# Local attention and a gated feed-forward block on one core: turns of x one tile ahead, turns of a batch inside its steps, output sums by thirds across tiles

## Chip, cores, metric

One core of one Trainium2 chip. The metric is the device time of that core in microseconds (us); quoted times are medians over the fast runs of a kernel, with their range. Unless another label is named, times inside an execution come from one profiled execution of each kernel, counted from its first instruction.

## The reference, cut to what matters

```python
# q, k, v: (8, 8, 576, 64) = batch, heads, rows, head width; 8 global positions
scores = q @ k.T / 8
mask = (abs(i - j) <= 32) | is_global[i] | is_global[j]
attn = softmax(where(mask, scores, -1e9))
x = (attn @ v).transpose(0, 2, 1, 3).reshape(4608, 512)
g = x @ w_gate                       # 512 -> 1536
val = x @ w_val
res_gate = sigmoid(x @ w_res)
out = x + res_gate * ((gelu(g) * val) @ w_out)
```

The kernel works through the 4608 rows in nine chunks of 512. While it runs the feed-forward block of chunk c, it computes the attention of chunk c+1. Each chunk has twelve steps j (a g product, a v product, Gelu, their product), then four output tiles of 128 rows. Rows of q and k are turned (transposed) before the scores; rows at the global positions are fetched by a gather with a list of indices. PSUM is where matmuls leave their results; a copy brings them out. In the traces, pt are the exponentials of the scores, masked by VectorE (DVE); ob is an output tile and prb the product that it is made from.

## The kernel before

The start of chunk 0. A step's products are begun for 128 rows as soon as that tile of x is turned:

```python
    values(0, 2)
    turn_x(0, 0)
    values(0, 3)
    begin(0)                       # g and v of steps 0 and 1 for 128 rows: 16 short matmuls
    for t in range(1, 4):
        turn_x(0, t)               # 4 transposes on TensorE into PSUM, one copy out
        begin(t)
```

GpSimd's list inside chunk 0 (issued at step 5) and the turns of batch 1:

```python
                    for n in (12, 13): cast_piece(n, POOL)      # pieces of the weights, f32 to bf16
                    for c5 in range(5): cast_v(1, c5, POOL)
                    for n in range(16, 20): load_piece(n)
                    for i, n in enumerate(range(14, 20)):
                        cast_piece(n, POOL)
                        if i % 2: shift_on_chip(i // 2)         # two GpSimd copies of v, moved by 64 rows
                    shift_on_chip(3)
                if 7 <= j < 11:
                    for what in "kq": turn_pair(1, j - 7, what) # behind step j, not inside it
```

The output tiles. `work_f[4*t]` is the gate of tile t, `work_f[4*t+1..3]` its thirds; the last third also makes the output:

```python
        def third(n):
            def emit():
                ...                                     # 4 of the 12 matmuls of f_ps
                if n == 2:
                    prb = work.tile([128, 512], F32, name="prb", tag="prb")   # the pool gives 2 buffers
                    nc.vector.scalar_tensor_tensor(prb, held["r"], 1.0, held["f"], ALU.add, ALU.mult)
                    ob = work.tile([128, 512], F32, name="ob", tag="ob")      # 2 buffers, too
                    nc.gpsimd.tensor_tensor(ob, prb, xtok[c % 2][:, t, :], ALU.add)
                    nc.sync.dma_start(out[r0:r0 + 128, :], ob)                # on SyncE's queue
```

The end of chunk 0, and the start of chunk 1:

```python
            load_second("k"); load_second("q")     # 10 loads of batch 2 on SyncE's queue
            ...
            work_f[3]()                            # output tile 0
            cast_second("q", 0, 1, POOL)
            values(1, 3)
            work_f[7]()                            # output tile 1
            cast_second("q", 1, 3, POOL)
            turn_qk(2, "k")                        # 5 DMA transposes on SyncE's queue
            turn_x(1, 2)
            work_f[9](); work_f[10]()
            turn_x(1, 3)
            work_f[11]()                           # output tile 2
            cast_second("q", 3, NQT, POOL)
            for n in (13, 14, 15): work_f[n]()     # output tile 3
    # chunk 1
            turn_qk(b, "q" if c == 1 else "qk")    # 5 DMA transposes on SyncE's queue
            load_v(b)                              # 5 DMAs issued by GpSimd
            if c in (1, 2, 4):
                for what in "kqv":
                    gather(what, c // 2 + 1)       # issued by GpSimd, behind load_v
    # chunk 1, steps 8 to 11
                    if j == 8: double_qk(n0, n1)   # casts of the gathered rows: kgd, qgd
                    elif j == 9:
                        got = turn_globals(n0, n1) # TensorE turns them: tg
                if j == 11: held = global_scores(b)   # sg
```

The softmax here doesn't subtract the row's maximum and nothing guards it: scores larger than these inputs give would overflow.

## Time and profile before

| | before |
|---|---|
| median of fast runs, us | 398.69 (397.61 to 399.43, 4 runs) |
| PE idle, 14 to 50 us | 4.03 |
| PE idle, 50 to 90 us | 1.91 |
| PE idle, 90 to 100 us | 0.21 |

The idle times are the length of a stretch less TensorE's (PE's) busy time in it, from the table by stretches.

### The profile page before, as it was taken

How to read it: one execution, taken by the hardware profiler on the slowest of the kernel's cores; microseconds unless marked ns; L12 is line 12 of the kernel's file. 1: busy time of each engine (PE TensorE's matmuls, PEld its weight loads, DVE VectorE, ACT ScalarE, POOL GpSimd, SP SyncE). 2: the span in 40 equal slices, each digit the busy share in tenths (PEclk: the TensorE clock that was granted, in tenths of full speed). 3: DMA queues.
4: the chain of work that ended last, by engine and by line, in shares of the span. 5: the costliest groups of instructions: out<-in, count | busy, mean ns of one | idle time of the engine just before them, and what ended most of it. 6: DMA issues, size and time to landing. Idle time of an engine off the chain costs nothing.

```text
span 396.5 us, 8446 instructions
## 1 busy us (share of the span) xinstructions
PE 376.3 (95%) x3309; PEld 196.4 (50%) x3360; DVE 204.2 (51%) x445; ACT 168.4 (42%) x279; POOL 172.1 (43%) x207
## 2 busy tenths in 40 slices
PE   3969998999999999999999999999999999999995
PEld 2655555444554455445544554455445544554443
DVE  7747668346643463456434553555445534553322
ACT  5744593236333643355234623372337233633320
POOL 7778678758247514461385226712501210121011
PEclk9999999999999999999999999999999999999999
DMA  8999999799439943998299929993990310041002
GB/s 241 222 360 366 246 337 212 164 162 176 59 109 155 189 58 99 119 202 85 79 156 161 115 81 115 194 108 86 112 147 16 80 55 0 2 96 52 0 29 79
DMA packets 153002, 52.78 MB, mean 133 GB/s; under 512 B 136386, under 2 KB 143426, under 8 KB 152962
## 3 DMA queue, kind: packets, MB, share of 16 engines
q1 hardware_dynamic: 77024, 41.88, 45.1%
q0 software_dynamic: 75392, 9.84, 42.4%
q8 instruction: 26, 0.43, 0.5%
q10 hardware_dynamic: 546, 0.52, 0.4%
q14 instruction: 14, 0.11, 0.1%
HBM read 39.19 MB, written 9.44 MB: 123 GB/s over the span
## 4 chain that ended last, share of the span: by engine, by line
PE 81%; DMA 5%; issue 5%; ACT 3%; DVE 3%; POOL 2%; SPq 0%; ACTq 0%; DVEq 0%; POOLq 0%
PE v_ps L618 21%; PE g_ps L618 21%; PE f_ps L661 20%; PE r_ps L636 6%; PE nd L563 4%; PE sc L523 2%; PE nd L575 2%; DMA qgf<-in_q_dram,idx 2%; DMA kt<-k_st 2%; DMA ht<-in_q_dram 1%; PE ss L477 1%; ACT pt L530 1%; POOL ob L667 1%; POOL ve L99 1%; DVE pt L545 1%
## 5 line engine op out<-in xcount | busy, mean ns | idle before, releaser
L625 DVE SCALAR_TENSOR_TENSOR ht<-gsb,v_ps 128x512 bf16<-128x512 bf16 x108 | 74.1, 687 | 97.4 <-PE v_ps L618 91.6
L624 ACT ACTIVATE gsb<-g_ps 128x512 bf16<-128x512 f32 x108 | 64.4, 597 | 125.5 <-PE g_ps L618 117.5
L667 POOL TENSOR_TENSOR ob<-prb,xtok 128x512 f32<-128x512 f32 x35 | 40.4, 1153 | 176.3 <-DVE prb L665 174.7
L618 PE MATMUL v_ps<-xt,wv_t 128*128 128x512 bf16 (+1 forms) x456 | 111.9, 368 | 0.4
L618 PE MATMUL g_ps<-xt,wg_t 128*128 128x512 bf16 (+1 forms) x438 | 109.6, 367 | 2.5 <-ACT xt L599 1.3
L661 PE MATMUL f_ps<-wo_t,ht 128*128 128x512 bf16 x395 | 97.8, 379 | 1.9 <-issue 1.0
L618 PEld LDWEIGHTS <-wg_t 128*128 128x128 bf16 x456 | 43.3, 98 | 50.6 <-issue 2.7
L618 PEld LDWEIGHTS <-wv_t 128*128 128x128 bf16 x456 | 43.5, 98 | 49.9
L661 PEld LDWEIGHTS <-ht 128*128 128x128 bf16 x420 | 38.8, 98 | 38.6
L639 ACT ACTIVATE rsb<-r_ps 128x512 bf16<-128x512 f32 x36 | 21.7, 607 | 71.0 <-PE r_ps L636 69.9
L530 ACT ACTIVATE pt<-sc 128x512 bf16<-128x512 f32 x72 | 37.5, 623 | 4.6 <-PE sc L523 4.6
L665 DVE SCALAR_TENSOR_TENSOR prb<-rsb,f_ps 128x512 f32<-128x512 bf16 x35 | 24.0, 686 | 28.4 <-PE f_ps L661 25.9
L636 PE MATMUL r_ps<-wr_t,xt 128*128 128x512 bf16 x136 | 36.2, 379 | 0.5
L545 DVE TENSOR_TENSOR pt<-pt,maskw 128x512 bf16<-128x512 bf16 x64 | 29.8, 481 | 8.1 <-ACT pt L530 6.1
L91 POOL DMA_DIRECT2D q_st<-in_q_dram x25 | 21.4, 866 | 19.6 <-DMA qt<-q_st 19.1
L563 PEld LDWEIGHTS <-pt 128*128 128x128 bf16 x576 | 22.0, 97 | 10.2 <-DVE pt L545 0.9
L99 POOL DMA_DIRECT2D ve<-in_v_dram x30 | 25.5, 864 | 0.0
L588 DVE TENSOR_TENSOR xtok<-nd,rden 128x512 bf16<-128x512 f32 x34 | 23.5, 692 | 1.3
L563 PE MATMUL nd<-ve,pt 128*128 128x65 bf16 x320 | 22.7, 193 | 0.6 <-DVE xtok L588 0.6
L91 POOL DMA_DIRECT2D k_st<-in_k_dram x25 | 21.1, 865 | 4.3 <-DMA kt<-k_st 3.4
L587 DVE RECIPROCAL rden<-nd 128x8 f32<-128x8 f32 x34 | 7.0, 207 | 28.1 <-PE nd L575 27.9
L563 PE MATMUL nd<-vo,pt 128*128 128x65 bf16 x256 | 20.1, 193 | 1.0 <-DVE pt L545 0.6
(166 smaller groups left out, 291.9 us busy)
## 6 DMA issues: line engine op xcount, KB each, us to landing
out_dram<-ob SPq DMA_DIRECT2D x35, 256.0 KB, 2.1
vo<-ve SPq DMA_DIRECT2D x12, 260.0 KB, 4.8
q_st<-in_q_dram POOLq DMA_DIRECT2D x20, 128.0 KB, 5.7
k_st<-in_k_dram POOLq DMA_DIRECT2D x20, 128.0 KB, 6.1
ve<-in_v_dram POOLq DMA_DIRECT2D x18, 128.0 KB, 7.1
wo_t<-in_k_dram SPq DMA_DIRECT2D x8, 256.0 KB, 6.8
vraw<-in_q_dram SPq DMA_DIRECT2D x8, 256.0 KB, 6.3
extra<-in_moe_w_out_dram SPq DMA_DIRECT2D x4, 512.0 KB, 6.7
```

The lines of the kernel that those rows point to most:

```text
L91: nc.gpsimd.dma_start(dst[0:n, r, :].rearrange("p (h d) -> p h d", d=D), src[b].rearrange("h s d -> s h d")[128 * r:128 * r + n])
L99: nc.gpsimd.dma_start(t[p0:p1, c, :, 0:D], v[b].rearrange("h s d -> s h d")[s0 + p0:s0 + p1])
L530: nc.scalar.activation(mine, sc, ACTF.Exp, bias=0.0, scale=SCALE)
L545: nc.vector.tensor_tensor(m, m, view(maskw, 0, 128, 64 * i0, [[0, 2], [64, 4], [1, 64]]), ALU.mult)
L563: nc.tensor.matmul(nds[h // 4][:, VG * (h % 4):VG * (h % 4) + VG], view(pt, 0, 128, c0, [[1, 128]]), vw, start=(h % 4 == 0 and e == 0), st ...
L618: nc.tensor.matmul(held[what][:, c0:c1], w[:, kk, 128 * j:128 * j + 128], x[:, kk, c0:c1], start=(kk == 0), stop=(kk == NKT - 1))
L624: nc.scalar.activation(gsb, held["g"], ACTF.Gelu, bias=0.0, scale=1.0)
L625: nc.vector.scalar_tensor_tensor(ht[:, j, :], gsb, 0.5, held["v"], ALU.mult, ALU.mult)
L636: nc.tensor.matmul(r_ps, xt[c % 2][:, kk, 128 * t:128 * t + 128], wr_t[:, kk, :], start=(kk == 0), stop=(kk == NKT - 1))
L661: nc.tensor.matmul(held["f"], ht[:, j, 128 * t:128 * t + 128], wo_t[:, j, :], start=(j == 0), stop=(j == NFF - 1))
L665: nc.vector.scalar_tensor_tensor(prb, held["r"], 1.0, held["f"], ALU.add, ALU.mult)
L667: nc.gpsimd.tensor_tensor(ob, prb, xtok[c % 2][:, t, :], ALU.add)
```

## The change

Three intents. Part 1: turn each tile of x one tile ahead, so that PE has 16 short matmuls to do while the copy out of PSUM runs; and begin the local values of tile 2 before the first tile's product with the globals. Part 2: the turns of batch 1 go inside steps 8 to 11, between g and v. Part 3: the thirds of the output sums go round the four tiles, so that PE has matmuls behind each tile's values; GpSimd's list is reordered so that v of batch 1 is whole earlier.

Core of the diff (a few changes of staging and PSUM places and of the loads' order, and an earlier start of the local values of batch 1's first tile, are cut):

```diff
+    begun_v.append(local_values(0, 2))
...
-    values(0, 2)
+    values(0, 2, begun_v[2])
     turn_x(0, 0)
     values(0, 3)
+    turn_x(0, 1)
     begin(0)
-    for t in range(1, 4):
-        turn_x(0, t)
-        begin(t)
+    turn_x(0, 2)
+    begin(1)
+    turn_x(0, 3)
+    begin(2)
+    begin(3)
...
+    turns = {8: lambda: turn(0), 9: lambda: turn(1), 10: lambda: turn(2), 11: lambda: turn(-1)}
+                ffn_in(c, j, turns.get(j) if c == 0 else None)
-                if 7 <= j < 11:
-                    for what in "kq":
-                        turn_pair(1, j - 7, what)
+                if j == 10:
+                    turn(3)
...
+                    for n in range(16, 20):
+                        load_piece(n)
                     for c5 in range(5):
                         cast_v(1, c5, POOL)
-                    for n in range(16, 20):
-                        load_piece(n)
-                    for i, n in enumerate(range(14, 20)):
+                        if c5 in (1, 2):
+                            shift_on_chip(c5 - 1)
+                    for n in range(14, 20):
                         cast_piece(n, POOL)
-                        if i % 2:
-                            shift_on_chip(i // 2)
+                        if n == 15:
+                            shift_on_chip(2)
                     shift_on_chip(3)
...
-            work_f[3]()
+            third(0, 1)
             cast_second("q", 0, 1, POOL)
             values(1, 3)
-            work_f[7]()
+            third(1, 1)
             cast_second("q", 1, 3, POOL)
             turn_qk(2, "k")
             turn_x(1, 2)
-            work_f[9]()
-            work_f[10]()
+            third(2, 1)
+            third(3, 1)
             turn_x(1, 3)
-            work_f[11]()
-            cast_second("q", 3, NQT, POOL)
-            for n in (13, 14, 15):
-                work_f[n]()
+            for t in range(4):
+                third(t, 2)
+                if t == 1:
+                    cast_second("q", 3, NQT, POOL)
```

In the last hunk all four output tiles now come behind `turn_qk(2, "k")`. Before, tiles 0 and 1 came ahead of it.

More of the change, by code (lines that the diff above doesn't have):

```diff
@@ L179 @@
     vplace = [[vraw[:, c, :] for c in range(5)],
-              [slots[2 + c // 2][:, 512 * (c % 2):512 * (c % 2) + 512] for c in range(5)]]
+              [slots[2 + c // 2][:, 512 * (c % 2):512 * (c % 2) + 512] for c in range(4)] + [wo32[:, 2560:3072]]]
     def load_vraw(b):
@@ L490, in global_rows @@
         e = b % 2
-        if b:
+        if b > 1:
             sn = psn.tile([128, 2, 512], F32, name="sn", tag="nd")[:, 0, 0:2 * VG]
@@ L734 @@
     ACT(vo[0][0:64, 2:4, :, :], ve[0][64:128, 2:4, :, :])
+    begun_v.append(local_values(0, 2))
     nc.scalar.activation(none, none, ACTF.Gelu, bias=0.0, scale=1.0)
-    fill(band, 1.0, [([[-1, 64]], 1, 0, ALU.is_ge, 0.0), ([[1, 64]], -1, 64, ALU.is_ge, 0.0)])
     for n in range(4):
@@ L741 @@
             load_piece(10 + n)
-    for p in (0, 1, 2, 3, -1):
+        else:
+            load_raw(1, "kq"[n - 2], 0, nc.sync)
+        if n == 1:
+            fill(band, 1.0, [([[-1, 64]], 1, 0, ALU.is_ge, 0.0), ([[1, 64]], -1, 64, ALU.is_ge, 0.0)])
+    for p in (1, 2, 3, -1):
         for what in "kq":
@@ L756, in begin, with turn @@
                 steps[what](128 * t, 128 * t + 128)
-    values(0, 2)
+    values(0, 2, begun_v[2])
     turn_x(0, 0)
     values(0, 3)
+    turn_x(0, 1)
     begin(0)
-    for t in range(1, 4):
-        turn_x(0, t)
-        begin(t)
+    turn_x(0, 2)
[3 more added lines that the diff above has]
+    begin(3)
     for steps in begun:
         steps["end"]()
+    def turn(p):
+        for what in "kq":
+            turn_pair(1, p, what)
+    turns = {8: lambda: turn(0), 9: lambda: turn(1), 10: lambda: turn(2), 11: lambda: turn(-1)}
     for c in range(NCH):
@@ L778 @@
             if c or j > 1:
-                ffn_in(c, j, (lambda: [turn_pair(1, -1, what) for what in "kq"]) if c == 0 and j == 11 else None)
+                ffn_in(c, j, turns.get(j) if c == 0 else None)
             if c == 0:
@@ L840, with third @@
         if c == 0:
+            def third(t, n):
+                work_f[4 * t + 1 + n]()
             global_exp(1, *global_scores(1))
@@ L851 @@
             cast_second("k", 0, NQT, ACT)
-            work_f[1]()
-            values(1, 0)
+            began = local_values(1, 0)
+            third(0, 0)
+            values(1, 0, began)
             mask(0, 2)
-            work_f[5]()
+            third(1, 0)
             values(1, 1)
             mask(2, 4)
-            work_f[2]()
+            third(2, 0)
             turn_x(1, 0)
-            work_f[6]()
+            third(3, 0)
             values(1, 2)
             turn_x(1, 1)
-            work_f[3]()
+            third(0, 1)
             cast_second("q", 0, 1, POOL)
             values(1, 3)
-            work_f[7]()
+            third(1, 1)
             cast_second("q", 1, 3, POOL)
```

## The prediction

> **What bounds the kernel now.** I read the page first: busy shares, the forty slices.
>
> ```profile
> span 396.5 us, 8446 instructions
> PE 376.3 (95%) x3309; PEld 196.4 (50%) x3360; DVE 204.2 (51%) x445; ACT 168.4 (42%) x279; POOL 172.1 (43%) x207
> PE   3969998999999999999999999999999999999995
> ```
>
> TensorE (PE) is the bound: nine tenths or more busy in nearly every slice, at full granted clock. Idle time worth taking lies only before about 75 us; after that the list of waits gives PE 1.3 us in all. So I listed PE's waits from 14 to 75 us (releaser: us in total, times, longest):
>
> ```profile
> PE g_ps L618 <- ACT xt L599: 1.3, 2, 0.7
> PE nd L575 <- DVE vgs L503: 0.8, 1, 0.8
> PE nd L563 <- DVE pt L545: 0.6, 1, 0.6
> PE g_ps L618 <- DVE xt L599: 0.5, 1, 0.5
> ```
>
> Rows one and four are the first steps: each waits until the turned tile of x has been copied out of PSUM. The timeline of one such round:
>
> ```profile
> 24.95 0.27 PEld L598 LDWEIGHTS <-xtok 128*128 128x128 bf16 x4
> 25.01 0.39 PE L598 MATMUL tx<-ident,xtok 128*128 128x128 bf16 x4
> 25.43 0.58 ACT L599 COPY xt<-tx 128x512 bf16<-128x512 bf16 x1 [1.96 <-PE tx L598]
> 26.07 0.38 PE L618 MATMUL g_ps<-xt,wg_t 128*128 128x128 bf16 x4 [0.67 <-ACT xt L599]
> ```
>
> From the turn's start to the first matmul that reads it is 1.06 us, of which PE issues for about 0.22.
>
> Last, because the change reorders queues, I read the timelines of SyncE's queue (SPq) and of POOL after the first chunk, and the landing of the gathers that the second chunk needs:
>
> ```profile
> 70.24 1.03 SPq L669 DMA_DIRECT2D out_dram<-ob  x2
> 71.88 6.73 SPq L466 DMA_TRANSPOSE kt<-k_st  x5
> 74.01 1.15 POOL L667 TENSOR_TENSOR ob<-prb,xtok 128x512 f32<-128x512 f32 x1 [1.61 <-DMA out_dram<-ob]
> 76.24 1.15 POOL L667 TENSOR_TENSOR ob<-prb,xtok 128x512 f32<-128x512 f32 x1
> 78.70 1.00 SPq L669 DMA_DIRECT2D out_dram<-ob  x2
> 79.75 7.62 SPq L466 DMA_TRANSPOSE qt<-q_st  x5
> 83.33 1.00 POOL L328 DMA_INDIRECT qgf<-in_q_dram,idx  x1 [0.30 <-issue]
> 90.27 0.22 DVE L397 CAST qgd<-qgf 128x128 bf16<-128x128 f32 x1
> ```
>
> The third output tile (74.01) may overwrite its buffer only when the first tile's output has left: there are two ob buffers. Behind the fourth (76.24) POOL issues load_v(2) and then the three gathers. The tile view of qgf gives 6.6 us from issue to landing: 83.33 + 6.6 = 89.93, read at 90.27. This path has about half a microsecond of slack today.
>
> **What the Trainium skill says.** "PSUM — Partial Sum Buffer", Engine vs sequencer instructions: the queues of ScalarE, VectorE and GpSimdE are strict FIFO, and matmuls run in program order. The trace agrees: POOL's gathers come behind its ob additions. "DMA: Bandwidth & Descriptors", Anatomy of one DMA: the DMA engines do not wait on semaphores; any wait is on the issuing sequencer. So one DMA of SPq that is slow to issue holds up every later one; here five transposes hold SPq for 6.73 us. The same page, Issuing engines are not separate DMA queues: all DMAs share 16 engines. The trace agrees: their share is 1.0 or more in every microsecond from 28 to 63, so nothing loaded there can be hurried by an earlier issue. "SBUF — State Buffer", Who interferes with whom: a DVE instruction with two SBUF inputs contends with a GpSimd one that reads SBUF; the masks take 874 ns each at 54 to 65 us beside POOL casts, against 481 on average.
>
> **Part 1, turns one tile ahead.** The order becomes turn(1), begin(0), turn(2), begin(1), turn(3), begin(2), begin(3). A begin is 0.88 us of PE, a turn 0.22; 1.10 covers the 1.06 of turn plus copy. The gaps from 25.18 to 26.07, 27.13 to 28.02 and 29.08 to 29.81 go: 0.89 + 0.89 + 0.73 = 2.5 us. Against it, local_values(0,2) now stands before the global product of tile 0, to fill the 0.8 us wait for vgs (20.95). But it reads vo, whose ScalarE copy runs 19.85 to 20.91. It can hardly begin earlier than that product, so its 16 matmuls (0.5 us) delay the DVE chain of reciprocals and products, which paces this stretch. Net: begin(3) ends at 28.85 in place of 30.70, about **1.9 us** won.
>
> **Part 2, turns of batch 1 inside steps.** The same instructions, moved inside the steps. At turn(3) and turn(-1) the ScalarE copy of q now precedes the Gelu, so ht and the k copy are some 0.4 us later and turn(-1) may wait that long for its PSUM bank. About **0.3 us** lost: global_scores(1) starts at about 49.0 in place of 50.66.
>
> **Part 3, thirds across tiles.** PE's work from 50.66 to 73.5 by my count: 48 f and 16 r matmuls at 0.216, 10.4 + 3.5; scores 2.2; values 3.6; turns 0.7; in all 20.4 of 22.9 us. So 2.5 us of stalls at most, 0.6 of them the mask wait. But the casts of the first w_out pieces end near 57.2 whatever PE does (POOL and DMA), so the earlier start makes PE wait there. With third(.,0) spread over the values I get g of chunk 1 at 71.6 to 71.7 instead of 73.5. To that point: **1.9 us faster** in all.
>
> **What it gives back.** In the old code the outputs of tiles 0 and 1 are queued on SPq before turn_qk(2,"k"). Now all four come after it. SPq must first issue the ten k and q loads, which the DMA engines hold back: the last ended at 70.13, and the only dips of their share, at 63 and 65 us, allow some 0.8 us earlier. So the k transposes start at about 69.7 and end at 76.4; output 0 is issued there and lands 3.4 to 3.6 later (the four landings of before are 3.4 to 4.1), at 80.0. Then ob 2 (1.15) and ob 3 (1.15) end at 82.3, in place of 77.39. load_v(2) and the gathers behind them move by 4.9 us, qgf lands at about 94.8, and the transposes of the global rows, at 90.97 now, can run at about 95.4. PE would be there at 89.1: it stalls 6 us, after winning 1.9. From there the rest is as it was, PE-bound, so nothing is recovered: 95.4 - 90.97 = 4.4; I take off 0.5 for lighter DMA traffic around the gathers: 398.45 + 3.9 = about **402.3 us**.
>
> **Rivals.** (a) The gain stays: if the transposes issue much faster, or the gathers land early because their queue is emptier, the stall shrinks to nothing and the time is 396.5. For: PE is the bound almost everywhere. Against: half a microsecond of slack in the gathers, and the two-buffer wait already stands in the trace with 1.6 us. The intent, plainly tuned, also speaks for it. (b) A wash: SPq is free earlier (68) and transposes issue at their minimum of 1.19 us each: output 0 at 74, gathers late by 2.5; 398.45 + 1.5 = 400. (c) Worse: the gathers now share the engines with the q transposes from their start, land 1.5 later still, and the second chunk's first steps wait for PSUM banks held by prb 2 and 3, which wait for the two prb buffers: 404.5.
>
> **Range and chances.** I give the give-back (main account, b, c) some 70% and (a) 30%. That puts the middle near 402 and the range from 396.2, the whole gain kept, to 404.6, rival (c). A 2% step is 8 us: a saving of that size isn't there, as the waits before 75 us sum to about 5; a loss of that size needs twice the delay that I work out.
>
> **What would show it.** Part 1: no g_ps wait on xt between 23 and 29 us, j=2 starting near 28.8. Part 3: fewer than 0.6 us waiting for pt, g of chunk 1 near 71.7. Give-back: SPq shows the five k transposes before any output; POOL waits 4 us or more for out_dram before its third ob; the gathers are issued near 87 to 90; PE waits 5 to 6 us for kgd or qgd near 89 to 95. If those gathers land before 89 us, the prediction is wrong and (a) is right.

## The result

After: 402.99 us (401.81 to 403.51, 4 runs). The ratio to before is 1.0106, 95% interval 1.0071 to 1.0141: slower by about 1%. Ratios here are the mean time of one kernel's fast runs over that of the other's of the same rounds, so they are not quite the ratio of the medians.

The changed kernel's page, to be set beside the three lines of before in the prediction (the last row here is the granted clock):

```profile
span 401.8 us, 8443 instructions
...
PE   3989989996999999999999999999999999999995
...
PEclk9999999998999999999999999999999999999999
```

The early dip at the third slice has become shallower, but the tenth slice (90 to 100 us) now has a 6, and the clock has an 8 there. In PE's idle time: 2.41 us from 14 to 50 us (before 4.03), 2.46 from 50 to 90 (before 1.91), and 3.97 from 90 to 100 (before 0.21). So the first part won, the third didn't, and a new hole opened.

| landmark, us from the start | before | after | after less before |
|---|---|---|---|
| vgs (values of the globals) done | 20.95 | 20.80 | -0.15 |
| step 2 begins | 30.88 | 28.82 | -2.06 |
| global_scores(1) | 50.66 | 48.78 | -1.88 |
| first g matmul of chunk 1 | 73.72 | 72.87 | -0.85 |
| output tile 0 issued | 70.24 | 77.37 | +7.13 |
| gather of the q rows issued (second of three) | 83.33 | 87.95 | +4.62 |
| second turn of global rows (tg) | 91.04 | 94.45 | +3.41 |
| global_scores of chunk 1 (sg) | 94.64 | 99.75 | +5.11 |
| end of span | 396.5 | 401.8 | +5.3 |

Read the last column downwards: 2 us won by 29 us, more than half of that lost by 73, all lost and more at 91 to 100, hardly anything after that (0.2).

**The beginning.** PE's timeline with ScalarE's copy beside it; columns are start, duration, engine, line, operation, output and inputs, count:

```profile
25.51 0.39 PE L598 MATMUL tx<-ident,xtok 128*128 128x128 bf16 x4
25.73 0.39 PE L618 MATMUL g_ps<-xt,wg_t 128*128 128x128 bf16 x4
25.93 0.58 ACT L599 COPY xt<-tx 128x512 bf16<-128x512 bf16 x1 [0.53 <-PE tx L598]
```

The turn is followed 0.22 us later by g matmuls of the tile before, and the copy runs beside them. The waits for xt are gone.

**The end of chunk 0.** The list of PE's waits of after, 14 to 78 us (total, times, longest):

```profile
PE nd L563 <- DVE pt L545: 1.3, 2, 0.8
```

The wait for pt was 0.6 before. VectorE's masks make pt; in this trace the longer wait is most of the 1.0 us lost between 49 and 73 us. Whether the change causes it is another question, taken up at E5 to E7.

**The queues.** SyncE's queue of after, 60 to 105 us:

```profile
70.33 6.95 SPq L466 DMA_TRANSPOSE kt<-k_st  x5
77.37 5.00 SPq L669 DMA_DIRECT2D out_dram<-ob  x4
82.42 6.61 SPq L466 DMA_TRANSPOSE qt<-q_st  x5
```

All five k transposes stand ahead of the first output. GpSimd (POOL), same stretch:

```profile
72.22 2.26 POOL L667 TENSOR_TENSOR ob<-prb,xtok 128x512 f32<-128x512 f32 x2
79.75 2.26 POOL L667 TENSOR_TENSOR ob<-prb,xtok 128x512 f32<-128x512 f32 x2 [4.16 <-DMA out_dram<-ob]
...
87.95 1.00 POOL L328 DMA_INDIRECT qgf<-in_q_dram,idx  x1 [0.30 <-issue]
```

The first two tiles are added at 72.22 and fill both buffers. The third waits 4.16 us for the first to leave, and the gathers stand behind it in POOL's order. PE at their end, after:

```profile
89.28 1.03 PE L618 MATMUL v_ps<-xt,wv_t 128*128 128x512 bf16 x4
93.78 0.23 PE L407 MATMUL tg<-ident,kgd 128*128 128x128 bf16 x1 [3.47 <-DVE kgd L397]
94.45 0.23 PE L407 MATMUL tg<-ident,qgd 128*128 128x128 bf16 x1 [0.44 <-DVE qgd L397]
94.51 1.66 PE L618 MATMUL g_ps<-xt,wg_t 128*128 128x512 bf16 x4
95.97 1.91 PE L618 MATMUL v_ps<-xt,wv_t 128*128 128x512 bf16 x4
...
99.75 0.43 PE L472 MATMUL sg<-qt,kgz 128*32 128x288 bf16 x8
```

And before:

```profile
90.99 0.22 PE L407 MATMUL tg<-ident,kgd 128*128 128x128 bf16 x1
91.10 1.03 PE L618 MATMUL g_ps<-xt,wg_t 128*128 128x512 bf16 x4
...
94.64 0.43 PE L472 MATMUL sg<-qt,kgz 128*32 128x288 bf16 x8
```

Two things are to be seen. PE stalls 3.47 + 0.44 us for the gathered rows. And behind the stall the same four g matmuls take 1.66 us, and the v matmuls 1.91, where they took 1.03. From the second turn to sg is 5.30 us after and 3.60 before: 1.70 us more for the same work. The table by stretches (stretch, length, busy time, count, granted clock, DMA share, GB/s), before:

```profile
90.00:100.00 10.00, 9.79 (x122) 1.00 2.06 168
```

After:

```profile
90.00:100.00 10.00, 6.03 (x27) 0.83 1.87 173
```

The clock was granted at 0.83 on average; in finer stretches it is 0.50 from about 94.8 to 98.1 us. I hadn't foreseen this. The Trainium skill has it: "TensorE: Matmul & The Clock Gate", What's actually happening, says that the clock drops to half after an idle window of about 3.4 us, that the window runs freely, and that it takes about as long a busy stretch to return. The trace agrees: 3.5 us of wait, then half the clock for 3.3 us, with 1.66 to 1.91 us for a group that takes 1.03.

### The profile page after: what moved, and what is told of

Read it like the earlier page. It is cut to its first block, busy times and chain, and to the rows that moved or that the text cites. A ratio compares the mean times of both kernels' runs of the same rounds, so it can differ in the third digit from the quotient of the medians.

```text
span 401.8 us, 8443 instructions
## 1 busy us (share of the span) xinstructions
PE 378.8 (94%) x3310; PEld 196.8 (49%) x3360; DVE 205.2 (51%) x445; ACT 168.1 (42%) x279; POOL 171.9 (43%) x207
## 4 chain that ended last, share of the span: by engine, by line
PE 76%; DMA 7%; DVE 5%; issue 5%; POOL 3%; ACT 3%; SPq 0%; DVEq 0%; POOLq 0%
PE f_ps L661 19%; PE v_ps L618 19%; PE g_ps L618 19%; PE r_ps L636 6%; PE nd L563 4%; PE sc L523 2%; DVE pt L545 2%; PE nd L575 2%; DMA kt<-k_st 2%; POOL ob L667 2%; DMA qgf<-in_q_dram,idx 2%; DMA vgf<-in_v_dram,idx 2%; DMA qt<-q_st 1%; ACT pt L530 1%; PE ss L477 1%
## 5 line engine op out<-in xcount | busy, mean ns | idle before, releaser
L661 PE MATMUL f_ps<-wo_t,ht 128*128 128x512 bf16 x395 | 98.1, 379 | 1.8 <-issue 0.8
L545 DVE TENSOR_TENSOR pt<-pt,maskw 128x512 bf16<-128x512 bf16 x64 | 30.9, 497 | 8.3 <-ACT pt L530 6.3
```

The costliest lines, as they stand in the source:

```text
L545: nc.vector.tensor_tensor(m, m, view(maskw, 0, 128, 64 * i0, [[0, 2], [64, 4], [1, 64]]), ALU.mult)
L661: nc.tensor.matmul(held["f"], ht[:, j, 128 * t:128 * t + 128], wo_t[:, j, :], start=(j == 0), stop=(j == NFF - 1))
```

## The experiments

**The theory.** The order alone makes the loss: the five transposes ahead of the outputs on SyncE's queue, with two ob buffers, hold POOL, so the gathers are late, PE stalls, and its clock drops. **Rivals:** (1) the late outputs also delay the q transposes and the prb buffers, so the time stays lost when the gathers no longer wait; (2) the loss lies in the three parts themselves, such as the slower masks; (3) the clock is a reading without a cost.

All were timed in five rounds, and all results were correct. The kernel before had a median of 398.89 (E1 to E4), 398.93 (E5 to E8) and 399.27 (E9 to E11).

| run | median, us | ratio to before (95%) |
|---|---|---|
| after | 402.99 | 1.0106 (1.0071 to 1.0141) |
| E1 after, gathers early | 399.55 | 1.001 (0.9978 to 1.0043) |
| E2 after, outputs 0 and 1 first | 397.74 | 0.9967 (0.9945 to 0.9989) |
| E3 before, transposes first | 403.03 | 1.0101 (1.007 to 1.0132) |
| E4 after, filler in the stall | 400.65 | 1.005 (1.0024 to 1.0076) |
| E5 E2, old POOL order | 398.39 | 0.9982 (0.9958 to 1.0007) |
| E6 E2, no early local values | 397.78 | 0.9982 (0.9959 to 1.0005) |
| E7 E5 and E6 together | 397.31 | 0.9963 (0.9938 to 0.9988) |
| E8 before, part 1 alone | 397.58 | 0.9972 (0.9949 to 0.9995) |
| E9 after, four ob buffers | 397.72 | 0.9962 (0.9947 to 0.9978) |
| E10 E3, gathers early | 399.04 | 0.9995 (0.9982 to 1.0009) |
| E11 E7, four ob buffers | 397.01 | 0.9947 (0.9935 to 0.996) |

### E1: the gathers out of the queue's reach

```diff
                     shift_on_chip(3)
+                    for what in "kqv":
+                        gather(what, 1)
...
-            if c in (1, 2, 4):
+            if c in (2, 4):
```

> The changed kernel with one edit: the three gathers of batches 2 and 3 are issued on POOL in chunk 0, behind the last on-chip shift, where POOL is idle for 3.9 us (64.4 to 68.3 in the trace of after), and no longer behind the four ob additions and load_v(2). Theory (the gathers, held up by SPq order, the two ob buffers and POOL order, make the loss): PE no longer waits for kgd at the ninth step of chunk 1, and the time falls by the stall of 4.2 us and what follows it, to 397.0 to 398.5, under the kernel before by up to 1 us. Rival 1 (the rest of the change is itself slower, or the transposes of q, issued at 82.4, bind next): 400 to 402. Rival 2 (the gathers are only where a loss elsewhere shows): 402 to 403 as before the edit.

Measured: 399.55 (396.69 to 400.59). The wait for gathered rows is gone (the second turn of global rows runs at 90.52), and 3.4 us of the median come back; the missed 397 to 398.5 shows that not all does. Outputs and q transposes are as late as in after (77.79 and 82.82), and two new short waits stand in PE's list:

```profile
PE g_ps L618 <- DVE prb L665: 0.7, 1, 0.7
PE sg L472 <- DMA qt<-q_st: 0.2, 1, 0.2
```

That is rival (1), with 0.9 us. The profile is of a run of 398.21; what holds the slower runs is not shown.

### E2: outputs 0 and 1 ahead of the transposes

```diff
             cast_second("q", 1, 3, POOL)
-            turn_qk(2, "k")
             turn_x(1, 2)
...
                 third(t, 2)
                 if t == 1:
+                    turn_qk(2, "k")
                     cast_second("q", 3, NQT, POOL)
```

> The changed kernel with the five k transposes of batch 2 queued on SPq behind the outputs of tiles 0 and 1, as the kernel before had them, all else as changed. Theory: output 0 leaves as soon as ob 0 is there (about 73.5, not 77.4), ob 3 ends near 79.3 in place of 82.0, so the gathers come 2.7 us earlier than in the changed kernel but still some 2 us later than in the kernel before (POOL casts q before its ob additions now): 399.5 to 400.5. Rival (the order on SPq does not matter, the length of the DMA backlog does): 402.5 to 403.5.

Measured: 397.74 (396.8 to 398.3), faster than I expected. SyncE's queue of E2:

```profile
72.55 1.47 SPq L669 DMA_DIRECT2D out_dram<-ob  x2
74.62 6.57 SPq L466 DMA_TRANSPOSE kt<-k_st  x5
```

The third addition runs at 74.73 without a wait, the gather of the q rows is issued at 82.98, and PE has no stall at 90. Moving one line takes 5.2 us off the median of after, so rival (2) can't be the main loss; nor can the edits that are cut from the diff above, as E2 keeps them.

### E3: the order alone, in the kernel before

```diff
+            turn_qk(2, "k")
             work_f[3]()
             cast_second("q", 0, 1, POOL)
             values(1, 3)
             work_f[7]()
             cast_second("q", 1, 3, POOL)
-            turn_qk(2, "k")
```

> The kernel before with one edit: the five k transposes of batch 2 are queued on SPq ahead of output 0, as in the changed kernel; nothing of parts 1 to 3. Theory (this order alone makes the loss): SPq starts the transposes near 70.2, output 0 leaves near 77, ob 3 ends near 82 in place of 77.4, the gathers land some 4.5 us later and PE waits at the ninth step of chunk 1: 402 to 404, by the order alone. Rival (the loss needs the earlier PE or the thirds): 398 to 399.5.

Measured: 403.03 (400.73 to 404.55). POOL of E3:

```profile
78.53 1.15 POOL L667 TENSOR_TENSOR ob<-prb,xtok 128x512 f32<-128x512 f32 x1 [7.21 <-DMA out_dram<-ob]
```

The third addition waits 7.21 us, and the gather of the q rows is issued at 87.85. With none of the three parts in it, the order gives the same ratio as the whole change (1.0101 against 1.0106). PE waits 2.2 + 0.5 us in this profile, and its clock stayed at 1.00: the profiled run is one of the quick ones (401.39). The two runs of at least 0.998 mean clock took 400.73 and 401.39; the four of 0.993 to 0.996 took 403.01 to 404.55. That fits a stall that sometimes does and sometimes doesn't cost the clock, but only the mean clock of those runs is known.

### E4: keep PE busy in the stall

```diff
                     elif j == 9:
+                        if c == 1:
+                            idle = psn.tile([128, 2, 512], F32, name="idle", tag="nd")
+                            for _ in range(16):
+                                nc.tensor.matmul(idle[:, 0, :], wr_t[:, 0, 0:128], wr_t[:, 0, :], start=True, stop=True)
                         got = turn_globals(n0, n1)
```

> The changed kernel with 16 matmuls of 512 columns (16 x 0.216 = 3.5 us) that nobody reads, put on PE just ahead of the turns of the global rows in chunk 1, where PE stood idle for 4.2 us. It tests why the first matmuls after that stall are slow (1.66 and 1.91 us for four in place of 1.03 in the trace of after). Theory (PE runs slowly after it has stood still for some 4 us, which costs about 1.5 us on top of the stall): with PE kept busy the matmuls behind the stall take 1.03 again and the time falls by 1.2 to 1.6 us, to 401.3 to 401.9, although work was added. Rival (they are slow for another reason, such as operands or the DMA load): unchanged, 402.5 to 403.5.

Measured: 400.65 (399.63 to 402.08), 2.35 us below after although PE has more to do. PE of E4:

```profile
93.41 0.22 PE L407 MATMUL tg<-ident,qgd 128*128 128x128 bf16 x1
93.47 1.03 PE L618 MATMUL g_ps<-xt,wg_t 128*128 128x512 bf16 x4
...
97.01 0.43 PE L472 MATMUL sg<-qt,kgz 128*32 128x288 bf16 x8
```

The g matmuls take 1.03 us again, and from the second turn to sg is 3.60 us, as before. So the clock did cost 1.70 us in after, and rival (3) falls. The gain is larger than the 1.2 to 1.6 that I expected; in E4's profile the k transposes also began at 68.07 instead of 70.33, so that execution's loads were earlier, and I can't give all of the 2.35 to the clock. The intervals of the two ratios just overlap, too, so it is the trace and not the total that carries this. E4's two slowest runs (401.68 and 402.08) still had a mean clock of 0.995.

### E5, E6, E7: what parts 1 and 3 cost beside the order

E5 takes E2 and puts the casts and shifts of chunk 0 back into the old order (the four loads stay early). E6 takes E2 and drops the early local values. E7 does both.

```diff
 E5:                 for c5 in range(5):
                         cast_v(1, c5, POOL)
-                        if c5 in (1, 2):
-                            shift_on_chip(c5 - 1)
-                    for n in range(14, 20):
+                    for i, n in enumerate(range(14, 20)):
                         cast_piece(n, POOL)
-                        if n == 15:
-                            shift_on_chip(2)
+                        if i % 2:
+                            shift_on_chip(i // 2)
 E6:
-    begun_v.append(local_values(0, 2))
-    values(0, 2, begun_v[2])
+    values(0, 2)
```

> E2 (changed kernel, k transposes behind the first two outputs) with the casts and on-chip shifts of POOL in chunk 0 back in the order of the kernel before (shifts behind the casts of w_out). In the changed kernel DVE's first four masks took 4.65 us in place of 3.52, and the first output sum began at 57.59 where I had worked out 56.75 to 57.2. Theory (the early shifts, which read and write SBUF, slow the masks on DVE and hold back the casts of w_out): the four masks take 3.5 to 3.8 us again, the first output sum starts 0.5 to 0.8 us earlier, and chunk 1 starts 0.3 to 0.8 us earlier than in E2; the time 397.0 to 397.6. Rival (the shifts are needed early for the values, or the masks are slowed by any POOL work): chunk 1 no earlier, 397.7 to 398.5.

> E2 with the local values of tile 2 back behind the global product of tile 1, the rest as E2. The prediction said that this early start cannot begin before the ScalarE copy of vo ends and so delays the DVE chain by about 0.5 us; in the trace of after the first reciprocal is 0.79 us behind vgs, in the kernel before 0.36. Theory: the first reciprocal comes 0.4 us earlier, the first steps end 0.3 to 0.5 us earlier than in the changed kernel (begin(3) near 28.1 in place of 28.5), and that moves global_scores(1) by as much; in the total 0 to 0.5 us, 397.3 to 397.8. Rival (early start fills a wait): the first steps end later, by up to 0.5 us.

> E5 and E6 together, as a candidate better than both kernels. Theory: the gains add up in the first chunk, chunk 1 starts 0.6 to 1.0 us earlier than in E2; but the gathers had only about half a microsecond of slack in E2, so a small wait for kgd can come back: 396.8 to 397.5. Rival: no faster than E2, 397.7.

Measured: E5 398.39 (397.13 to 398.61), E6 397.78 (396.86 to 398.51), E7 397.31 (396.22 to 398.2). Against E2's 397.74 none differs: the intervals overlap. E5 missed its 397.0 to 397.6 and lies in its rival's range. The four first masks in before, by source line (minimum, median and longest in ns, first and last start):

```profile
L545 DVE TENSOR_TENSOR pt<-pt,maskw x4: 412/1042/1253, 54.6 to 57.3; 128x512 bf16<-128x512 bf16 x4
```

In after:

```profile
L545 DVE TENSOR_TENSOR pt<-pt,maskw x4: 425/758/2795, 52.7 to 54.5; 128x512 bf16<-128x512 bf16 x4
```

And in E7:

```profile
L545 DVE TENSOR_TENSOR pt<-pt,maskw x4: 425/426/1112, 52.9 to 54.4; 128x512 bf16<-128x512 bf16 x4
```

Beside after's long mask, from 54.5 us on, POOL ran these:

```profile
54.30 0.80 POOL L190 CAST ve<-wo_t 96x512 bf16<-96x512 f32 x1
55.04 2.02 POOL L145 CAST wo_t<-extra 128x1024 bf16<-128x1024 f32 x2
```

One mask spans three POOL casts. The four masks together take 4.65 us in after, 3.52 in before and 2.58 in E7. Over all profiles these times go with POOL's order: 3.67 to 4.80 us in the six kernels with the new order, 1.90 to 3.57 in the seven with the old one.

But E5, whose masks take 3.57, isn't faster in total. E7 shows a reason. Its first output sum starts at 56.80, without a wait (57.59 in after), but PE then waits 0.29 and 0.94 us for later masks, at 62.78 and 63.96; two of these take 2.28 us together beside POOL's casts from 61.41 on, where after's took 1.17. The list of E7's waits:

```profile
PE nd L563 <- DVE pt L545: 1.2, 2, 0.9
```

That is the 1.3 of after again, with the old order. E8, below, has 1.5 with the old order, and E2 0.2 with the new one. So the first masks are longer with the new order, but that it costs PE time is not shown: the wait for pt moves to other masks and varies from one profiled execution to the next. E5's own profile fell on an execution with a low clock in its first steps, so its total remains inconclusive.

For the early local values: from the end of vgs to step 2 is 8.02 us in after and 7.58 in E6 and in E7, so they cost 0.44 us there. The first reciprocal comes 0.79 us behind vgs instead of 0.36.

### E8: part 1 alone, in the kernel before

```diff
+    begun_v.append(local_values(0, 2))
-    values(0, 2)
+    values(0, 2, begun_v[2])
     turn_x(0, 0)
     values(0, 3)
+    turn_x(0, 1)
     begin(0)
-    for t in range(1, 4):
-        turn_x(0, t)
-        begin(t)
+    turn_x(0, 2)
+    begin(1)
+    turn_x(0, 3)
+    begin(2)
+    begin(3)
```

> The kernel before with part 1 alone (turns of x one tile ahead of the first steps, with the early local values), nothing of parts 2 and 3, order on SPq as before. Theory: the first steps end 2.0 to 2.2 us earlier (28.5 in place of 30.7), global_scores(1) starts 1.9 to 2.2 earlier, but by the start of chunk 1 some of it is lost to the casts of w_out, the masks and the shifts, which do not depend on PE, and the gathers, which keep their time, allow about 0.5: the total 397.6 to 398.6, a gain of 0 to 1 us. Rival 1 (the whole gain goes through): 396.5 to 397. Rival 2 (an earlier PE alone makes the loss seen in the changed kernel): 400 or more.

Measured: 397.58 (397.01 to 399.07), ratio 0.9972. From the end of vgs to the first g matmul of chunk 1 is 52.77 us in before, 52.46 in E8, 50.90 in E2. So in E8's trace part 1's 1.9 us are nearly all waited off again before chunk 1: PE waits 1.5 us there for pt (0.6 in before) and 0.8 for POOL's casts of the weights (none in before). In E2 they are kept, but after itself, with 52.07, keeps only 0.7. The total agrees with E2's within the intervals, so I claim no more than that part 1 alone isn't worth its whole 1.9 us.

### E9: four ob buffers

```diff
-                    ob = work.tile([128, 512], F32, name="ob", tag="ob")
+                    ob = work.tile([128, 512], F32, name="ob", tag="ob", bufs=4)
```

(in both places that make an ob)

> The changed kernel with four ob buffers in place of two, the order on SPq and POOL as changed. Theory (the chain runs over the buffer: output 0 leaves late, so ob 2 may not start, so load_v(2) and the gathers behind it are late): POOL no longer waits 4.2 us for out_dram, ob 3 ends near 78 in place of 82, the gathers come 4 us earlier, PE waits for kgd or qgd at most 1 us, and the time falls to 397.6 to 399.0. Rival (SPq alone holds the gathers up, or the q transposes bind next as in E1): 399.5 to 403.

Measured: 397.72 (396.4 to 398.33). SyncE's queue of E9, which keeps after's order:

```profile
69.61 6.95 SPq L466 DMA_TRANSPOSE kt<-k_st  x5
76.65 2.15 SPq L669 DMA_DIRECT2D out_dram<-ob  x4
```

POOL of E9:

```profile
74.93 2.26 POOL L667 TENSOR_TENSOR ob<-prb,xtok 128x512 f32<-128x512 f32 x2
```

The outputs still leave late, but nobody waits for them: the third addition runs at 74.93, the gather of the q rows is issued at 83.15, and the stall at 90 us is gone. So the late queue does its harm through the two buffers; no other cost is seen.

### E10 and E11: the gathers in E3, and the best parts together

E10 is E3 with the edit of E1. E11 is E7 with the edit of E9.

> E3 (the kernel before with the k transposes ahead of output 0) with the gathers of E1 issued early, in chunk 0 behind the last on-chip shift. Theory (in E3 too the gathers are the only path by which the order costs time): no wait for kgd at the ninth step of chunk 1; what stays is the q transposes on SPq some 2.5 us later, which may make global_scores(2) wait up to 0.7 us, as in E1: 398.6 to 400.0 against 403.0 of E3. Rival (another path): 401 or more.

> E7 with four ob buffers, as a last candidate. With the outputs first, ob 2 hardly waited for out_dram in E7, so theory: no difference that five rounds can tell, 397.0 to 397.8. Rival (a wait for the buffer is left that the trace put down to something else): 396.5 or less.

Measured: E10 399.04 (398.37 to 399.96), ratio 0.9995. The outputs and q transposes are as late as one expects with the order of E3 (75.84 and 81.99), but the second turn of global rows runs at 91.46 without a wait, and the 1% is gone. So in E3 the gathers are the whole path. E11: 397.01 (396.47 to 397.62), ratio 0.9947 (0.9935 to 0.996). It is faster than both kernels, by 2 us against before and some 6 against after, which was not timed in the same rounds. It is not shown to be faster than E2 or E9, whose intervals overlap its own.

## Why the prediction was right, and where its sum was off

- **The give-back** held link by link. The transposes ahead of the outputs: start 70.33 for 69.7, end 77.28 for 76.4. POOL's wait for out_dram: 4.16 us for "4 us or more". The fourth addition done at 82.01 for 82.3, but here two errors cancel: output 0 left 1.0 us later than I said (77.37 for 76.4) and let the third addition start after 2.4 us, where I had counted 3.6. The gathers issued from 86.57 to 89.26 for 87 to 90, the q rows used at 94.16 for 94.8. E2 and E3 show that the order makes it, E9 that it goes through the two buffers, E1 and E10 that it goes through the gathers.
- **Part 1** held: 1.91 us won, from the end of vgs to step 2 (9.93 to 8.02), for 1.9; step 2 starts at 28.82 for 28.8. The 0.5 us for the early local values measures 0.44 in E6 and E7.
- **Part 2**: from step 2 to global_scores(1) 19.96 us instead of 19.78, so 0.2 lost for 0.3.
- **Part 3** is the term that was mis-sized. I put g of chunk 1 at 71.6 to 71.7, counted to its weight load; it came near 72.66, counted the same way (before 73.51). The lead was 0.85 us, not 1.9. In after's trace PE waited 1.3 us for pt where I had said fewer than 0.6, the longer of the two waits (0.81) just ahead of the first output sum. The first four masks grew from 3.52 to 4.65 us beside POOL's casts; I had named this contention in the part on the skill and hadn't priced it. But E7 and E8 wait as long with POOL's old order, so that the reorder cost the lead is not shown. What is shown is that these waits, which I took to shrink, came in both orders.
- **The stall** was 3.9 us, not 5 to 6: PE came to it at 90.31 instead of 89.1, as the lead was smaller, and the rows came at 94.2 instead of 94.8. From there to the turn took 0.3 us, where I had let 0.6 pass. The delay of the second turn was 3.4 us, for 4.4.
- **The clock** was missing from the sum: 1.70 us, shown by E4. The terms close: 3.41 + 1.70 = 5.11, which is sg's delay, and the span differs by 5.3.
- **The total**, 402.99 for 402.3, is right partly because errors cancel: a delay 1.0 us too large, of which 0.5 was taken off again for lighter traffic, and a clock cost of 1.7 left out, and the profiled pair differs by 5.3 us where the medians differ by 4.3. The mechanism was right; a match to 1 us in the sum is luck. The range, 396.2 to 404.6, held every rival too, so it is the traces and not the total that tell them apart. Two small slips of the text change nothing: from 50.66 to 73.5 is 22.8 us, not 22.9, and the DMA share was 0.99, just under 1.0, from 52 to 53 us.
- **The rivals.** (a) fell in after, but E2, E9 and E11 are what it would have been: 397.0 to 397.7, where it said 396.5. (b) fell: SyncE's queue was free at 70.33, not 68, and output 0 left at 77.37, not 74. (c) named the prb buffers and later q transposes; E1 shows these waits, with 0.9 us.

## What to carry to other kernels

When a change moves small outputs behind slow issues on an in-order queue, follow the chain to its end: queue, buffers of the output tile, the engine that fills them, what that engine issues next, and the slack of whoever reads that; here, with half a microsecond of slack, gathers issued 4.6 us later became a stall of 3.9 us. Put the outputs ahead or give them more buffers; both are changes of one or two lines and each took 5 us off. A stall of PE like this one (3.5 us) should be priced with a stretch of lower clock behind it, and a reorder of POOL with what DVE does in the same microseconds.

## What the Trainium skill lacked or had wrong

- "SBUF — State Buffer", Who interferes with whom: it says that a DVE instruction with two SBUF inputs contends with a GpSimd one that reads SBUF, and the masks agree. It gives no size for this form. Here one mask took 2795 ns where the shortest of its group took 425, over three POOL casts in a row (0.80, 1.01 and 1.01 us), so it lost far more than one instruction's time.
- "DMA: Bandwidth & Descriptors": no duration is given for which the issue of a 128x512 bf16 transpose between SBUF tiles holds SyncE's queue. Here (before and after together) one took 1.19 to 1.51 us for k and 1.21 to 2.00 us for q, while four plain outputs took 2.15 us in E9.
- "TensorE: Matmul & The Clock Gate", What's actually happening: the idle window of about 3.4 us that it gives fits after's wait of 3.5 us, but isn't the whole condition, and the page doesn't say how busy is busy enough. In E5's profile the clock fell to 0.50 from about 23.9 to 27.3 us although PE was busy 1.90 of the 3.40 us before and no single wait there was over 0.63 us. In after PE was about as busy around that point (1.87 of 3.40 us) and the clock stayed at 1.00; in E3 waits of 2.2 and 0.5 us left it at 1.00.
